# Generation's parameters in turns, ten stored pieces for twelve, and a newly searched order

## The chip, the cores and the metric

One core of a Trainium2 chip. The metric is the device time of one execution in microseconds; a run is one execution. The program is straight-line: every engine (TensorE, here PE, with its weight loads PEld; VectorE, DVE; ScalarE, ACT; GpSimd, POOL; and SyncE, SP, which issues DMAs) has its own list of instructions and takes them in order, and semaphores make one wait for another.

## The reference

Two mixers over the same x (2048 positions of 640 channels), blended by a gate.

```
g = sigmoid((x * gate_w).sum(-1))
# a: attention, 32 heads of 20; each position sees itself and 7 earlier ones, 2 apart
qkv = x @ wqkv;  a = softmax(q . k[s - 2w] / sqrt(20)) . v[s - 2w], w = 0..7;  a = a @ wo
# b: a long convolution whose filter comes from 640 x 192 complex modes
dt = exp(log_dt)
K[d, l] = Re sum_n C[d,n] * exp(dt[d] * A[d,n] * l) * dt[d] * B[d,n]
b = irfft(rfft(x, 4096) * rfft(K, 4096))[:2048] + x * Dskip
out = g * a + (1 - g) * b
```

For each mode, the kernel needs logarithm and angle of the weight C B dt, and the rates dt A_re and dt A_im.

## The kernel before

**Start.** The inputs are loaded. `SSMParams.build` computes the parameters on tiles of 128 partitions x 960 (five channels of 192 modes each), on DVE and ACT: the weight wr, wi; its log size xl; its angle at by an arc tangent of the smaller over the larger of |wr| and |wi|, followed by three corrections by octant; the phase per step tau; the decay per step xa. Each result is split into bf16 pieces that add up to it (`piece`: ACT copies to bf16, the DMA on SP stores it to Sprm in DRAM, DVE subtracts it from the value, and so on). Beside this PE transposes x (`turn`, evicted by `tev`) and makes q, k and v (`late`, five matmuls of 512 columns for one 128 x 512 tile, evicted by `lev` on ACT or DVE). At most two such tiles are open at a time (tb has two buffers).

**Generation.** `KGen` loads pieces from Sprm into L (`L0S` on SP and `L0G` on POOL for the first of ten chunks of channels) and multiplies L by a table of constants Rarg (`arg`, on PE): this gives the arguments of sine and exponential for 32 + 2 x 22 or 32 + 22 steps. The sine's argument is wanted modulo one turn: a large constant (MAGIC) is added in the same matmul, so that the low 16 bits of the f32 sum are the phase in units of 1/65536 turn, read as int16. ACT takes the sine (`act`, scaled by 2 pi / 65536) and the exponential; DVE multiplies them (`pq`), and PE sums over the modes with dense small matmuls (`kmm`), evicted by `fin`. Beside it runs the attention in eight blocks of 256 positions: loads of qc, kc, vc on POOL, products on DVE (`prod`, `pv`), sums on PE (`lg`, `gat`), the exponential on ACT, the output projection (`wo`, evicted by `ga`). POOL also loads rows of x (Usb) for the FFT.

**FFT.** The filter is expanded and both it and x are transformed (`f1`, `fk`, `fu`); then comes `fft_conv`, with a plan of its own, "tail", which the change leaves as it is.

**Order.** Every step is a task of a `Plan`. The string `ORDER["main"]` gives the sequence of all tasks as differences of their numbers, with a letter where a task runs on the engine that isn't its first choice. `Plan.emit` records the tasks in that sequence, and each engine keeps it. It was found by a search, outside of the kernel.

Of the kernel before, what the change touches and what calls it, by code (L numbers as in the profile page):

```python
# [10 lines left out]
ACT = mybir.ActivationFunctionType  # L11
ALU = mybir.AluOpType
# [8 lines left out]
S = 2048  # L21
# [16 lines left out]
def _attn_consts():  # L38
# [443 lines left out]
def _arg_consts():  # L482


    i = np.arange(KI)
    m = np.array(MS)
    sp = np.zeros((64, 4, KI), np.float32)
    sq = np.zeros((64, 4, 2, NM), np.float32)
    ep = np.zeros((64, 4, KI), np.float32)
    eq = np.zeros((64, 4, NM), np.float32)  # L490
    for qq in range(4):
        r = 2 + qq * NPC
        for j in range(3):
            sp[r + j, qq] = 8.0 * i - 124.0
            sq[r + j, qq] = (m % 256)[None]
            sq[r + 5 + j, qq] = (m // 256)[None]
        for j in range(2):
            ep[r + 3 + j, qq] = 8.0 * i
            eq[r + 3 + j, qq] = m
            sq[r + 8 + j, qq] = 1.0  # L500
            eq[r + 10 + j, qq] = 0.5
# [17 lines left out]
class SSMParams:  # L519
# [5 lines left out]
    def build(self, ctx, tc, pl, A_re, A_im, B_re, B_im, C_re, C_im, log_dt, gate_w, at_, pa, xl, wl):  # L525
# [25 lines left out]
        dt2 = pin.tile([128, 5], F32, name="dt2")  # L551
# [11 lines left out]
        for c in (MAGIC, -MAGIC * 65536.0, 1e-36, float(-np.pi / 2)):  # L563
# [8 lines left out]
        def tt(name, o, a, b, alu, rdy=0.0):  # L572
            ap = lambda n: dtB if n == "dtb" else dt2[:].unsqueeze(2).to_broadcast(SH) if n == "dt2" else t[n][:]
# [19 lines left out]
        def wrap(dst, src, mul, tmp):  # L593
            lin(tmp, src, mul / 65536.0, MAGIC)
            lin(tmp, tmp, 65536.0, -MAGIC * 65536.0)
            stt(dst, src, float(mul), tmp, ALU.mult, ALU.subtract)

        def piece(cur, nxt, i):
            k = f"pc{i}"

            def make(_):
                t[k] = pcs.tile(SH, BF16, name="pc")
                SCA.activation(t[k][:], t[cur][:], ACT.Identity)
            op(f"mk{i}", "A", 0.9, make, [cur], [k], acq=["pc"])
# [4 lines left out]
        def split(src, i0, n):  # L609
            bufs = [src, "s0", "s1"][:n] + [None]  # L610
# [723 lines left out]
```

## Time and profile before

| | |
|---|---|
| runs (3) | 351.91, 352.40 and 354.79 us, median 352.4 |
| the profiled execution | 354.43 us |
| its span, first to last instruction | 352.4 us |
| mean granted clock of TensorE | 0.972 |
| busy: PE, DVE, ACT, POOL | 305.6, 307.8, 306.1, 86.6 us |
| table loads of ACT in the first 65 us | 6, each 1.283 us |

Times in the profile are microseconds from the first instruction. A row of the timeline has its start, its length, the engine (SPq and POOLq are the queues that issue DMAs), the line, the operation, output <- inputs, shapes, and the count merged in it; in brackets stands how long the engine had been idle and who released it. "issue" means that it waited for nothing that the profile shows.

### The profile page before, as it was taken

To read this page: it belongs to the slowest core of one execution; us is meant where nothing else is said; L and a number is where in the kernel's file an instruction comes from. 1 tells how busy PE (TensorE), PEld (TensorE's weight loads), DVE (VectorE), ACT (ScalarE), POOL (GpSimd) and SP (SyncE) were. 2 spreads that over 40 slices of the span, in tenths; PEclk is the share of its full clock that TensorE was granted. 3 is DMA by queue.
4 is the path that set the end of the run, shared out by engine and by line. 5 is a ranking of instruction groups with operands and counts; after the bars stand their busy time and mean duration, and the time that the engine had idled before them with its cause. 6 is when DMAs were issued, how large, how long until landed. Compare 5 with 4: busy or idle time off the path is not lost. (4 is left out here: it accounts for less than half of the span.)

```text
span 352.4 us, 11782 instructions
## 1 busy us (share of the span) xinstructions
PE 305.6 (87%) x5051; PEld 182.0 (52%) x5094; DVE 307.8 (87%) x421; ACT 306.1 (87%) x460; POOL 86.6 (25%) x110
## 2 busy tenths in 40 slices
PE   0598989999999999999999699999889989997860
PEld 0444544444454455444545255566567866666750
DVE  5999989889999989999999499999667879999982
ACT  2999983899999999999999499988687979998991
POOL 8912303132030030001413333574011000000052
PEclk9999999999999999999999699999999999998995
DMA  8965685557266074206696594625338236566046
GB/s 261 360 191 154 182 243 138 152 174 233 79 171 227 13 232 134 50 14 190 206 322 168 114 283 123 172 76 162 124 120 264 87 131 196 144 133 113 4 118 182
DMA packets 43373, 56.76 MB, mean 161 GB/s; under 512 B 19514, under 2 KB 35194, under 8 KB 43322
## 3 DMA queue, kind: packets, MB, share of 16 engines
q1 hardware_dynamic: 35136, 30.96, 30.6%
q0 software_dynamic: 7440, 24.45, 23.8%
q8 instruction: 39, 0.64, 0.7%
q10 hardware_dynamic: 746, 0.61, 0.6%
q14 instruction: 12, 0.10, 0.1%
HBM read 36.24 MB, written 19.77 MB: 159 GB/s over the span
## 5 line engine op out<-in xcount | busy, mean ns | idle before, releaser
L288 PE MATMUL tb<-bufA 128*128 128x512 bf16 x273 | 75.2, 392 | 8.0 <-issue 2.9
L752 ACT ACTIVATE big<-ar 128x608 bf16<-128x608 int16 x96 | 59.0, 682 | 6.5 <-PE ar L740 5.2
L740 PE MATMUL ar<-Rarg,L 64*128 64x304 bf16 (+1 forms) x480 | 52.5, 279 | 5.4 <-issue 3.0
L754 ACT ACTIVATE big<-ar 128x864 bf16<-128x864 f32 x60 | 50.3, 920 | 0.1
L336 DVE TENSOR_TENSOR prod<-qc,kc 128x2048 bf16<-128x2048 bf16 x40 | 47.9, 1219 | 2.2 <-PE lg L342 2.0
L402 DVE TENSOR_TENSOR pv<-vc,asb 128x2048 bf16<-128x2048 bf16 x40 | 48.4, 1219 | 1.4 <-PE tb L408 1.3
L288 PEld LDWEIGHTS <-bufA 128*128 128x128 bf16 x300 | 31.6, 122 | 34.7 <-issue 17.1
L791 PEld LDWEIGHTS <-pt 128*32 128x32 bf16 (+1 forms) x2560 | 25.3, 92 | 29.8 <-issue 22.2
L408 PE MATMUL tb<-pv,ident 128*128 128x512 bf16 (+1 forms) x176 | 37.9, 341 | 1.6 <-issue 1.3
L791 PE MATMUL kps<-qq,pt 128*32 128x22 bf16 (+1 forms) x2560 | 36.2, 173 | 1.7 <-issue 1.3
L740 PEld LDWEIGHTS <-L 64*128 64x128 bf16 x480 | 20.7, 94 | 27.7 <-issue 23.0
L774 DVE TENSOR_TENSOR pt<-big 128x1024 bf16<-128x1024 bf16 x48 | 32.2, 686 | 1.6 <-PE kps L791 0.6
L431 PE MATMUL tb<-wo_sb,oT 128*128 128x320 bf16 x160 | 30.7, 311 | 1.3 <-ACT ga L440 1.3
L1126 POOL DMA_DIRECT2D out_dram<-ot x14 | 7.7, 558 | 70.7 <-PE yp L1099 68.8
L458 ACT ACTIVATE sp_u<-fp 128x640 bf16<-128x640 f32 x31 | 23.5, 929 | 0.8 <-PE fp L1008 0.8
L408 PEld LDWEIGHTS <-ident 128*128 128x128 bf16 x192 | 17.0, 98 | 13.1 <-issue 1.6
L458 ACT ACTIVATE sp_k<-fp 128x640 bf16<-128x640 f32 x29 | 22.5, 960 | 1.1 <-PE fp L1008 1.1
L458 ACT ACTIVATE big<-bp 128x1024 bf16<-128x1024 f32 x17 | 16.8, 1026 | 5.7 <-PE bp L1235 5.6
L776 DVE TENSOR_TENSOR qq<-big 128x1408 bf16<-128x1408 bf16 x24 | 21.2, 885 | 0.0
L938 POOL COPY pace<-Usb 32x2 bf16<-32x2 bf16 x7 | 13.9, 1989 | 24.7 <-DMA Usb<-in_A_x_dram 24.7
L458 ACT ACTIVATE prj<-tb 128x512 bf16<-128x512 f32 x25 | 15.5, 618 | 5.1 <-PE tb L288 5.1
L1008 PEld LDWEIGHTS <-PHI 128*128 128x128 bf16 x160 | 15.5, 97 | 8.1 <-issue 1.1
(177 smaller groups left out, 582.9 us busy)
## 6 DMA issues: line engine op xcount, KB each, us to landing
asb<-aS SPq DMA_DIRECT2D x8, 512.0 KB, 4.3
Sprm<-pc SPq DMA_DIRECT2D x12, 240.0 KB, 4.3
L<-Sprm SPq DMA_DIRECT2D x76, 36.0 KB, 2.4
kc<-kS POOLq DMA_DIRECT2D x8, 337.5 KB, 4.8
vc<-vS POOLq DMA_DIRECT2D x8, 337.5 KB, 6.2
xn<-in_A_x_dram SPq DMA_DIRECT2D x4, 640.0 KB, 6.1
qc<-qS POOLq DMA_DIRECT2D x8, 320.0 KB, 4.1
gaS<-ga SPq DMA_DIRECT2D x8, 320.0 KB, 2.5
```

Of the source, the lines that this page charges most:

```text
L288: nc.tensor.matmul(ppf, self.wq[:, which, kt, e::5], self.xT[:, c0 // 1024, kt, c0 % 1024:c0 % 1024 + SC], start=(kt == 0), stop=(kt == NK ...
L336: nc.vector.tensor_tensor(b[e][:], b["qc"][:, e, :].unsqueeze(1).to_broadcast([128, W, C]), win(b["kc"][:, e, :], 0, W, DIL, C), ALU.mult)
L402: nc.vector.tensor_tensor(b["pv", e][:, :, k, :].rearrange("p w (b t) -> p w b t", t=64), for_e, aw, ALU.mult)
L408: nc.tensor.matmul(b["op", e][:, 0:n, :], ident[:], b["pv", e][:, w, 0:n, :], start=(w == 0), stop=(w == W - 1))
L431: nc.tensor.matmul(apf[:, :320], b["oT"][:, e, i * 128:(i + 1) * 128], wo_sb[:, e, hf * 320:(hf + 1) * 320], start=(e == 0), stop=(e == 4))
L458: nc.scalar.activation(o, i, ACT.Identity)
L740: nc.tensor.matmul(ar[:, g2, a0:a0 + ncol], L[rows, sb, gp, l0:l0 + 128], R[rows, c0:c0 + ncol], start=True, stop=True, tile_position=(64 ...
L752: nc.scalar.activation(dst[:, 2 * gp:2 * gp + 2, sub, :], ar[:].bitcast(I16)[:, :, 0:2 * SW:2], ACT.Sin, scale=SCL)
L754: nc.scalar.activation(dst[:, 2 * gp:2 * gp + 2].rearrange("p g s n -> p g (s n)"), ar[:, :, 0:2 * EW], ACT.Exp)
L774: nc.vector.tensor_tensor(pt[:, :, k, :], gg[:, :, ::-1] if k else gg, e1, ALU.mult)
L776: nc.vector.tensor_tensor(qq[:], trg[:, :, KI:].rearrange("p a (v m) -> p a v m", v=2), exq[:, :, KI:].unsqueeze(2).to_broadcast([128, 32, ...
L791: nc.tensor.matmul(kps[32 * g:32 * g + 32, h, NM * ql:NM * ql + NM], pt[rows, k, v, :], qq[rows, k, v, :], start=(g not in started), stop= ...
```

## The change

The unit of the phase becomes a turn. dt is multiplied once by 1/(2 pi) (`dtc`, 128 x 5), so that the phase is in turns from the start, and "modulo one turn" is: add and subtract MAGIC in one pass, and subtract (`nearest`). `wrap`, two passes and a third, goes, and so does the separate split of 256 tau (`x1`). The phase's pieces are digits of fixed units, 2^-8, 2^-16, 2^-24, each made by DVE by adding and subtracting MAGIC times the unit (`digit`), and a fourth piece for what is left; the other pieces (two each of xl, xa and at) are made by ACT or DVE. The log size takes dt in as lnd, half the logarithm of the size being added to it. The angle comes from the half angle: wi / (|w| + |wr|), with |w| = exp(0.5 ln |w|^2) and the division as exp(-ln); one correction instead of three. Rarg's rows are arranged to match, and ten pieces are stored per mode instead of twelve. `ORDER["main"]` is new; each of its places differs.

```
-NPC = 12
+NPC = 10
...
-        for j in range(3):
-            sp[r + j, qq] = 8.0 * i - 124.0
-            sq[r + j, qq] = (m % 256)[None]
-            sq[r + 5 + j, qq] = (m // 256)[None]
+        for j in range(4):
+            sp[r + j, qq] = 65536.0 * (8.0 * i - 124.0)
+            sq[r + j, qq] = 65536.0 * (m if j else m % 256)[None]
...
-        def wrap(dst, src, mul, tmp):
-            lin(tmp, src, mul / 65536.0, MAGIC)
-            lin(tmp, tmp, 65536.0, -MAGIC * 65536.0)
-            stt(dst, src, float(mul), tmp, ALU.mult, ALU.subtract)
+        def nearest(o, a, unit):
+            c = MAGIC * unit
+            op(f"near_{o}", "D", 0.62, lambda _: V.tensor_scalar(t[o][:], t[a][:], c, c, ALU.add, ALU.subtract), [a], [o])
+
+        def digit(cur, nxt, i, unit):
+            k, c = f"pc{i}", MAGIC * unit
+
+            def make(_):
+                t[k] = pcs.tile(SH, BF16, name="pc")
+                V.tensor_scalar(t[k][:], t[cur][:], c, c, ALU.add, ALU.subtract)
+            op(f"mk{i}", "D", 0.62, make, [cur], [k], acq=["pc"])
+            op(f"sp{i}", "S", 0.36, lambda _: nc.sync.dma_start(Sv[:, :, i, :], t[k][:]), [k], [f"S{i}"], dma=1.1)
+            op(f"rs{i}", "D", 1.07, lambda _: V.tensor_tensor(t[nxt][:], t[cur][:], t[k][:], ALU.subtract), [cur, k], [nxt])
...
-            op(f"mk{i}", "A", 0.9, make, [cur], [k], acq=["pc"])
+            op(f"mk{i}", "AD", {"A": 0.9, "D": 0.62}, make, [cur], [k], acq=["pc"])
...
         def phase():
-            tt("tau", "tau", "aim", "dtb", ALU.mult, rdy=9.6)
-            wrap("tau", "tau", U16, "s0")
-
-        def ratio():
-            stt("t0", "ax", 1e-30, "ay", ALU.max, ALU.max)
...
-            tt("s0", "s0", "t0", "s1", ALU.mult)
-            stt("t0", "s0", 2.0, "s1", ALU.subtract, ALU.mult)
-            tt("t1", "t1", "ax", "ay", ALU.min)
-            stt("t1", "t1", -1.0, "t0", ALU.mult, ALU.mult)
-            act("at", "t1", ACT.Arctan, "atan")
+            tt("tau", "tau", "aim", "dtc", ALU.mult, rdy=9.6)
+            nearest("x1", "tau", 1.0)
+            tt("tau", "tau", "tau", "x1", ALU.subtract)
...
+        def half():
+            op("act_ay", "A", 0.9, lambda _: SCA.activation(t["ay"][:], t["xl"][:], ACT.Exp, scale=0.5), ["xl"], ["ay"], table="exp")
+            tt("ay", "ay", "ay", "ax", ALU.add)
+            op("act_t0", "A", 0.9, lambda _: SCA.activation(t["t0"][:], t["ay"][:], ACT.Ln, bias=bias[1e-36]), ["ay"], ["t0"], table="ln")
+            op("act_t1", "A", 0.9, lambda _: SCA.activation(t["t1"][:], t["t0"][:], ACT.Exp, scale=-1.0), ["t0"], ["t1"], table="exp")
+            tt("t1", "t1", "wi", "t1", ALU.mult)
+            act("at", "t1", ACT.Arctan, "atan")
+            op("stt_xl", "D", 1.07, lambda _: V.scalar_tensor_tensor(t["xl"][:], t["xl"][:], 0.5, lnd[:].unsqueeze(2).to_broadcast(SH), ALU.mult, ALU.add), ["xl", "lnd"], ["xl"])
...
+        def digits():
+            for i, (a, b) in enumerate((("tau", "s0"), ("s0", "s1"), ("s1", "s0"))):
+                digit(a, b, i, 2.0 ** (-8 * i - 8))
+            piece("s0", None, 3)
...
-        for step in [weights, phase, squares, st[0], ratio, size, st[1], st[2], lambda: wrap("x1", "tau", 256.0, "t0"), sl[0], sl[1], angle1, sx[0],
-                     sx[1], angle2, sx[2], lambda: tt("xa", "xa", "are", "dtb", ALU.mult, rdy=19.0), sa[0], angle3, sa[1], sp[0], sp[1]]:
+        for step in [weights, phase, size, half, digits, lambda: two("xl", "ax", 8), angle, start, lambda: two("at", "x1", 6),
+                     lambda: tt("xa", "xa", "are", "dtb", ALU.mult, rdy=19.0), lambda: two("xa", "ay", 4)]:
```

What the new order does to the engines' lists is shown at three places. The first is the head of DVE's list (wr, wi: the weight; tau: the phase; dt and dtc: the small tiles made from dtb, which ACT makes from log_dt). Before:

```order
L574 TENSOR_TENSOR wr<-cre,bre 128x960 [waits DMAHW1_49,DMAHW0_49]
L574 TENSOR_TENSOR t_144<-cim,bim 128x960 [waits DMAHW3_49,DMAHW2_49]
L574 TENSOR_TENSOR wr<-wr,t_144 128x960 [waits DVE_49]
L624 TENSOR_TENSOR dt_139<-dtb 128x5 [waits Activation_49]
L574 TENSOR_TENSOR t_145<-cim,bre 128x960
L574 TENSOR_TENSOR tau<-aim,dtb 128x960 [waits DMAHW0_49]
```

and now:

```order
L628 TENSOR_SCALAR dtc<-dtb 128x5 [waits Activation_49]
L573 TENSOR_TENSOR wr<-cre,bre 128x960 [waits DMAHW1_49,DMAHW0_49]
L573 TENSOR_TENSOR t_145<-cim,bim 128x960 [waits DMAHW3_49,DMAHW2_49]
L573 TENSOR_TENSOR t_146<-cim,bre 128x960
L573 TENSOR_TENSOR wr<-wr,t_145 128x960 [waits DVE_49]
```

The small tile, which waits for ACT, moved from fourth place to the first. The second place is the end of the parameters on DVE (pc: a piece; at: the angle; prj: a tile of q, k or v; prod: the first block's products). Before:

```order
L607 TENSOR_TENSOR s_155<-xa,pc 128x960 [waits DVE_49,Activation_49]
L460 CAST prj<-tb 128x512 [waits DMAHW6_49,DMAHW7_49,DMAHW1_49,PE_49]
L580 SCALAR_TENSOR_TENSOR at<-at,t_145 128x960 [waits Activation_49]
L460 CAST prj<-tb 128x512 [waits PE_49]
L607 TENSOR_TENSOR s_155<-at,pc 128x960 [waits Activation_49]
```

and now:

```order
L573 TENSOR_TENSOR at<-at,t_145 128x960 [waits DVE_49]
L460 CAST pc<-at 128x960 [waits DMAHW2_49,DVE_49]
L615 TENSOR_TENSOR x_152<-at,pc 128x960 [waits DVE_49]
L460 CAST pc<-x_152 128x960 [waits DMAHW5_49,DMAHW1_49,DVE_49]
L460 CAST prj<-tb 128x512 [waits DMAHW7_49,DMAHW6_49,PE_49]
```

The last pieces are now made by DVE itself, where each step waited for ACT. The third place is the first argument matmul in PE's list (lg: the first block's logits, hi and lo the two halves of minus its maximum, at its exponentials; bufA: the weights of q, k, v). Before:

```order
L370 MATMUL lg<-at,ident 128x64
L288 LDWEIGHTS bufA
L288 MATMUL tb<-bufA 128x512
L740 LDWEIGHTS L_165
L740 MATMUL ar<-Rarg,L_165 128x304
```

and now:

```order
L362 MATMUL lg<-hi,ident 128x512
L362 LDWEIGHTS ident
L362 MATMUL lg<-lo,ident 128x512
L288 LDWEIGHTS bufA
L288 MATMUL tb<-bufA 128x512
L743 LDWEIGHTS L_162
L743 MATMUL ar<-Rarg,L_162 128x304
```

The first block's sum over exponentials, which stood ahead of the argument, now stands behind it, and so do 20 more of the L288 matmuls: 122 of them are ahead of it where 142 were. ACT's list has 461 instructions for 469, DVE's 415 for 423; ACT_TABLE_LOAD stands on ACT 19 times for 17.

More of the change, by code (lines that the diff above doesn't have):

```diff
@@ L467 @@
 MAGIC = 12582912.0
-U16 = 65536.0 / (2.0 * np.pi)
 CQ = 8
 NCH = 80 // CQ
-NPC = 12
+NPC = 10
 KI = 32
@@ L492, in _arg_consts @@
         r = 2 + qq * NPC
-        for j in range(3):
-            sp[r + j, qq] = 8.0 * i - 124.0
-            sq[r + j, qq] = (m % 256)[None]
-            sq[r + 5 + j, qq] = (m // 256)[None]
+        for j in range(4):
+            sp[r + j, qq] = 65536.0 * (8.0 * i - 124.0)
+            sq[r + j, qq] = 65536.0 * (m if j else m % 256)[None]
         for j in range(2):
[L498 to L501, printed above, removed]
+            ep[r + 4 + j, qq] = 8.0 * i
+            eq[r + 4 + j, qq] = m
+            sq[r + 6 + j, qq] = 65536.0
+            eq[r + 8 + j, qq] = 1.0
     sp[0] = MAGIC; sq[0] = MAGIC
@@ L550, in build @@
         dtb = pin.tile([128, 5], BF16, name="dtb")
-        dt2 = pin.tile([128, 5], F32, name="dt2")
+        dtc = pin.tile([128, 5], F32, name="dtc")
+        lnd = pin.tile([128, 5], F32, name="lnd")
         dtB = dtb[:].unsqueeze(2).to_broadcast(SH)
@@ L562, in build @@
         bias = {}
-        for c in (MAGIC, -MAGIC * 65536.0, 1e-36, float(-np.pi / 2)):
+        for c in (1e-36, 0.5):
             bc = pin.tile([128, 1], F32, name=f"bc{len(bias)}")
@@ L572, in tt @@
         def tt(name, o, a, b, alu, rdy=0.0):
-            ap = lambda n: dtB if n == "dtb" else dt2[:].unsqueeze(2).to_broadcast(SH) if n == "dt2" else t[n][:]
+            ap = lambda n: dtB if n == "dtb" else dtc[:].unsqueeze(2).to_broadcast(SH) if n == "dtc" else t[n][:]
             op(name, "D", 1.07, lambda _: V.tensor_tensor(t[o][:], ap(a), ap(b), alu), [a, b], [o], rdy=rdy)
@@ L591, in lin, with make @@
             op(f"lin_{o}", "AD", {"A": 0.9, "D": 0.62}, fn, [a], [o])
-        def wrap(dst, src, mul, tmp):
-            lin(tmp, src, mul / 65536.0, MAGIC)
-            lin(tmp, tmp, 65536.0, -MAGIC * 65536.0)
-            stt(dst, src, float(mul), tmp, ALU.mult, ALU.subtract)
+        def nearest(o, a, unit):
[9 more added lines that the diff above has]
+            op(f"rs{i}", "D", 1.07, lambda _: V.tensor_tensor(t[nxt][:], t[cur][:], t[k][:], ALU.subtract), [cur, k], [nxt])
         def piece(cur, nxt, i):
             k = f"pc{i}"
-            def make(_):
+            def make(e):
                 t[k] = pcs.tile(SH, BF16, name="pc")
-                SCA.activation(t[k][:], t[cur][:], ACT.Identity)
-            op(f"mk{i}", "A", 0.9, make, [cur], [k], acq=["pc"])
+                evict(nc, e, t[k][:], t[cur][:])
+            op(f"mk{i}", "AD", {"A": 0.9, "D": 0.62}, make, [cur], [k], acq=["pc"])
             op(f"sp{i}", "S", 0.36, lambda _: nc.sync.dma_start(Sv[:, :, i, :], t[k][:]), [k], [f"S{i}"], dma=1.1)
@@ L607, in piece @@
                 op(f"rs{i}", "D", 1.07, lambda _: V.tensor_tensor(t[nxt][:], t[cur][:], t[k][:], ALU.subtract), [cur, k], [nxt])
-        def split(src, i0, n):
-            bufs = [src, "s0", "s1"][:n] + [None]
-            return [lambda i=i: piece(bufs[i], bufs[i + 1], i0 + i) for i in range(n)]
         for n_, v in zip(("t0", "t1", "wr", "wi", "ax", "ay", "tau", "x1", "xa", "xl", "at", "s0", "s1"), (t0, t1, wr, wi, ax, ay, tau, x1, xa, xl_, at, s0, s1)):
@@ L622, in weights @@
             tt("wi", "wi", "wi", "t1", ALU.add)
-            act("ay", "wi", ACT.Abs)
-            op("dt2", "D", 0.16, lambda _: V.tensor_tensor(dt2[:], dtb[:], dtb[:], ALU.mult), [], ["dt2"])
+            op("dtc", "D", 0.12, lambda _: V.tensor_scalar(dtc[:], dtb[:], float(0.5 / np.pi), None, ALU.mult), [], ["dtc"])
         def phase():
-            tt("tau", "tau", "aim", "dtb", ALU.mult, rdy=9.6)
-            wrap("tau", "tau", U16, "s0")
-        def ratio():
-            stt("t0", "ax", 1e-30, "ay", ALU.max, ALU.max)
-            op("act_s0", "A", 0.9, lambda _: SCA.activation(t["s0"][:], t["t0"][:], ACT.Ln), ["t0"], ["s0"], table="ln")
-            op("act_s1", "A", 0.9, lambda _: SCA.activation(t["s1"][:], t["s0"][:], ACT.Exp, scale=-1.0), ["s0"], ["s1"], table="exp")
-            tt("s0", "s0", "t0", "s1", ALU.mult)
-            stt("t0", "s0", 2.0, "s1", ALU.subtract, ALU.mult)
-            tt("t1", "t1", "ax", "ay", ALU.min)
-            stt("t1", "t1", -1.0, "t0", ALU.mult, ALU.mult)
-            act("at", "t1", ACT.Arctan, "atan")
@@ L640, in squares, with size @@
-        def squares():
+            tt("tau", "tau", "aim", "dtc", ALU.mult, rdy=9.6)
+            nearest("x1", "tau", 1.0)
+            tt("tau", "tau", "tau", "x1", ALU.subtract)
+        def size():
             act("xl", "wr", ACT.Square)
             act("xa", "wi", ACT.Square)
-        def size():
             tt("xl", "xl", "xl", "xa", ALU.add)
-            tt("xl", "xl", "xl", "dt2", ALU.mult)
             op("act_xl", "A", 0.9, lambda _: SCA.activation(t["xl"][:], t["xl"][:], ACT.Ln, bias=bias[1e-36]), ["xl"], ["xl"], table="ln")
-        def angle1():
-            tt("t0", "t0", "ay", "ax", ALU.is_gt)
-            stt("t1", "at", float(np.pi / 4), "t0", ALU.subtract, ALU.mult)
-            stt("at", "t1", -2.0, "at", ALU.mult, ALU.add)
@@ L654, in angle2 @@
-        def angle2():
-            lin("t1", "at", 1.0, float(-np.pi / 2))
-            stt("t1", "wr", 0.0, "t1", ALU.is_lt, ALU.mult)
-            stt("at", "t1", -2.0, "at", ALU.mult, ALU.add)
-        def angle3():
-            stt("t1", "wi", 0.0, "at", ALU.is_lt, ALU.mult)
-            stt("at", "t1", -2.0, "at", ALU.mult, ALU.add)
-            lin("t0", "tau", 124.0, 0.0)
-            stt("at", "at", float(U16), "t0", ALU.mult, ALU.add)
-            wrap("at", "at", 1.0, "t1")
-        st, sx, sa, sl, sp = split("tau", 0, 3), split("x1", 5, 3), split("xa", 3, 2), split("xl", 10, 2), split("at", 8, 2)
@@ L666, in build @@
-        for step in [weights, phase, squares, st[0], ratio, size, st[1], st[2], lambda: wrap("x1", "tau", 256.0, "t0"), sl[0], sl[1], angle1, sx[0],
-                     sx[1], angle2, sx[2], lambda: tt("xa", "xa", "are", "dtb", ALU.mult, rdy=19.0), sa[0], angle3, sa[1], sp[0], sp[1]]:
+            op("lnd", "A", 0.24, lambda _: SCA.activation(lnd[:], dtb[:], ACT.Ln), [], ["lnd"], table="ln")
+        def half():
[6 more added lines that the diff above has]
+            op("stt_xl", "D", 1.07, lambda _: V.scalar_tensor_tensor(t["xl"][:], t["xl"][:], 0.5, lnd[:].unsqueeze(2).to_broadcast(SH), ALU.mult, ALU.add), ["xl", "lnd"], ["xl"])
@@ new lines, in angle, with start @@
+        def angle():
+            lin("t1", "at", -2.0 / np.pi, 0.5)
+            stt("t1", "wr", 0.0, "t1", ALU.is_lt, ALU.mult)
+            stt("at", "at", float(1.0 / np.pi), "t1", ALU.mult, ALU.add)
+        def start():
+            stt("at", "tau", 124.0, "at", ALU.mult, ALU.add)
+            nearest("t0", "at", 1.0)
+            tt("at", "at", "at", "t0", ALU.subtract)
+        def digits():
+            for i, (a, b) in enumerate((("tau", "s0"), ("s0", "s1"), ("s1", "s0"))):
+                digit(a, b, i, 2.0 ** (-8 * i - 8))
+            piece("s0", None, 3)
@@ L668, in build, with two @@
+        def two(src, rest, i):
+            piece(src, rest, i)
+            piece(rest, None, i + 1)
+        for step in [weights, phase, size, half, digits, lambda: two("xl", "ax", 8), angle, start, lambda: two("at", "x1", 6),
+                     lambda: tt("xa", "xa", "are", "dtb", ALU.mult, rdy=19.0), lambda: two("xa", "ay", 4)]:
             step()
```

86 rows, old and new, of the table ORDER are left out of this document.

## The prediction

> **What bounds the kernel now.** First the busy shares of the page, then a table of the span in stages, then the timeline of the first 65 us.
>
> ```profile
> PE 305.6 (87%) x5051; PEld 182.0 (52%) x5094; DVE 307.8 (87%) x421; ACT 306.1 (87%) x460; POOL 86.6 (25%) x110
> ```
>
> Three engines stand at the same 87%, so the average names no bound. By stage (length, then busy us and instructions of PE, its weight loads, DVE, ACT, POOL, then the granted clock, DMA share and GB/s):
>
> ```profile
> 20.00:30.00 10.00, 8.72 (x41) 4.43 (x41) 9.54 (x11) 9.94 (x13) 1.35 (x2) 1.00 0.40 121
> 30.00:40.00 10.00, 8.81 (x61) 5.33 (x62) 9.72 (x10) 10.00 (x15) 1.76 (x2) 1.00 0.77 229
> 40.00:50.00 10.00, 8.78 (x109) 5.34 (x109) 8.68 (x10) 9.21 (x12) 2.60 (x3) 1.00 0.84 225
> 50.00:60.00 10.00, 9.38 (x54) 3.99 (x54) 9.79 (x17) 4.15 (x6) 3.21 (x5) 1.00 0.43 101
> 65.00:85.00 20.00, 19.07 (x172) 7.84 (x172) 16.91 (x24) 19.78 (x28) 6.76 (x8) 1.00 0.65 192
> 85.00:105.00 20.00, 18.96 (x436) 9.70 (x440) 18.41 (x27) 19.13 (x32) 3.87 (x5) 1.00 0.51 139
> 105.00:125.00 20.00, 18.81 (x472) 9.72 (x477) 18.86 (x25) 19.53 (x30) 0.85 (x1) 1.00 0.41 139
> 125.00:145.00 20.00, 19.54 (x457) 10.75 (x462) 19.38 (x23) 19.88 (x33) 3.50 (x4) 1.00 0.56 161
> 145.00:165.00 20.00, 19.13 (x382) 10.12 (x382) 19.29 (x26) 19.82 (x35) 1.58 (x2) 1.00 0.18 49
> 165.00:185.00 20.00, 18.59 (x389) 9.86 (x392) 18.95 (x36) 19.94 (x30) 5.79 (x7) 1.00 0.84 275
> 185.00:205.00 20.00, 16.59 (x373) 8.06 (x374) 13.91 (x20) 14.56 (x27) 6.50 (x11) 0.83 0.64 153
> ```
>
> From 65 to 185 us ACT is idle for 1.9 us of 120 and PE for 5.9: this stretch, in which the filter is generated, is full. From 20 to 50 ACT and DVE are nearly full with the parameters while PE loses 3.7 us; from 50 to 60 ACT is busy for 4.15 only. So what a faster parameter stage is worth is read from where generation starts:
>
> ```profile
> 50.80 1.00 ACT L603 ACTIVATE pc<-s 128x960 bf16<-128x960 f32 x1 [1.55 <-DMA Sprm<-pc]
> 55.75 4.64 SPq L712 DMA_DIRECT2D L<-Sprm  x10
> 63.39 0.43 PE L740 MATMUL ar<-Rarg,L 64*128 64x304 bf16 x4
> 65.07 7.32 ACT L752 ACTIVATE big<-ar 128x608 bf16<-128x608 int16 x12
> 282.82 0.70 PE L1008 MATMUL fp<-bufA,PHI 128*128 128x320 bf16 x4 [0.91 <-ACT bufA L458]
> ```
>
> The last piece is made at 51.80, the tables L are fetched 3.95 us later, the first argument matmul stands at 63.39 and the first sine at 65.07. The FFT part, whose order is not changed, starts at 282.82: the middle is 219.4 us long.
>
> **The change, part by part.** DVE's parameter instructions first: a three-operand pass when it needs nothing new, when it needs the result just in front of it, and a one-source pass.
>
> ```profile
> 9.00 1.15 DVE L574 TENSOR_TENSOR tau<-aim,dtb 128x960 f32<-128x960 bf16 x1
> 10.07 1.15 DVE L574 TENSOR_TENSOR wi<-cre,bim 128x960 f32<-128x960 bf16 x1
> 23.66 1.15 DVE L574 TENSOR_TENSOR s<-t,s 128x960 f32<-128x960 f32 x1
> 24.85 1.16 DVE L580 SCALAR_TENSOR_TENSOR t<-s,s 128x960 f32<-128x960 f32 x1
> 27.24 0.66 DVE L588 TENSOR_SCALAR t<-tau 128x960 f32<-128x960 f32 x1
> 27.93 0.66 DVE L588 TENSOR_SCALAR t<-t 128x960 f32<-128x960 f32 x1
> 14.02 1.22 DVE L460 CAST bufA<-ar 128x1024 bf16<-128x1024 f32 x1
> 22.00 0.69 DVE L460 CAST pv<-tb 128x512 bf16<-128x512 f32 x1
> ```
>
> Start to start that is 1.07, 1.19 and 0.58 to 0.69 us; I use 1.11 and 0.63. Before, DVE has 33 passes with a second tensor and 4 with one source; after, 23 and 10 (a nearest integer twice, three digits, one line, four copies to bf16): 10 x 1.11 less and 6 x 0.63 more, **7.3 us less on DVE**. The three digits and four copies write bf16 from f32 in SBUF, a form that this trace does not show. Bounds: 0.63 like the f32 passes here, 1.15 like the eviction of 1024 f32 above, scaled to 960. Source and size are those of the 0.63 rows, so I take that; at the upper end the seven cost 3.6 us more. The Trainium skill (VectorE: DVE Perf Modes, "The perf-mode tier table") says that one-source passes on f32 in SBUF run at twice the rate of two-source passes and that any PSUM operand drops a tier; 0.66 against 1.15 us here agrees, and by it the lower bound is the right one.
>
> ACT made all 12 pieces and half of the lines: 24 passes before, 11 after. One costs 0.90 start to start, and a table load 1.30:
>
> ```profile
> 18.02 1.28 ACT L632 ACT_TABLE_LOAD   x1
> 19.32 1.00 ACT L632 ACTIVATE s<-t 128x960 f32<-128x960 f32 x1
> 24.00 0.99 ACT L603 ACTIVATE pc<-xl 128x960 bf16<-128x960 f32 x1
> 24.90 0.59 ACT L458 ACTIVATE pv<-tb 128x512 bf16<-128x512 f32 x1
> 6.75 0.21 ACT L553 ACTIVATE dtb<-ldt 128x5 bf16<-128x5 bf16 x1 [2.26 <-DMA ldt<-in_B_log_dt_dram]
> ```
>
> 13 x 0.90 goes, 2 x 1.30 comes since logarithm and exponential now take turns (ln, exp, ln, exp, arc tangent where it was ln, exp, arc tangent): **9.1 us less on ACT**. The Trainium skill (ScalarE: Activation LUTs, "What ACT_TABLE_LOAD costs") speaks against this edit: it puts a change of table set at 2.66 us, a drain included, so two more would be 5.3 us and the arc tangent 2.7 us later. Here the pass starts 1.30 us after the load did, and no drain is seen; I give that rule 2 in 100, at 346.7 + 2.7 = 349.4.
>
> Now the chain to the first argument matmul. The changed order puts dtc, which needs dtb, **first** on DVE; before, three large passes stood ahead of the small one. dtb is ready at 6.96, held by its load, so DVE's first pass starts at 7.1 and not at 4.41: a new wait of 2.7 us with all of DVE behind it. From there DVE has 23 x 1.11 + 10 x 0.63 + the large eviction at 1.13 + four small ones at 0.60 (the row of 0.69 less the 0.08 by which all of these overlap) = 35.4, and the last piece is ready at 42.5; I add 0.7 for late5's eviction, whose PE work cannot start before ACT's fourth large eviction at about 18.4. That is 43.2 against 51.8. ACT is not later: from the square of wi at 14.75 to the end of the arc tangent stand 8 passes and 3 large evictions at 0.90, 4 table loads at 1.30 and 6 small evictions at 0.48, 18.0 us, so 32.8 and some 34 with short waits for PE; DVE by its own sum needs the arc tangent at 34.1. With ten stores for twelve and L cut from 48 to 40 rows, nothing on SP grows; I count that as nothing, hidden under DVE's passes. L at 43.2 + 3.95 = 47.2, its landing some 4 us later.
>
> Three things then meet at the first argument:
>
> ```profile
> 50.48 2.35 DVE L336 TENSOR_TENSOR prod<-qc,kc 128x2048 bf16<-128x2048 bf16 x2
> 59.59 0.23 DVE L358 SCALAR_TENSOR_TENSOR lo<-mx,hi 128x64 bf16<-128x64 f32 x1
> 17.14 3.57 PE L288 MATMUL tb<-bufA 128*128 128x512 bf16 x8 [0.84 <-ACT bufA L458]
> 60.46 2.32 PE L288 MATMUL tb<-bufA 128*128 128x512 bf16 x10
> ```
>
> - L itself: about 51.5.
> - DVE: the new order has the first block's softmax maximum ahead of the argument on PE. From the first product to that maximum's low part took 59.82 - 50.48 = 9.3 us with two evictions among it that now stand in front: 43.2 + 9.3 = 52.5, and a microsecond of PE: 53.5.
> - PE: ten matmuls of 512 took 2.32 us with their drain, 0.216 each. PE had 142 of them ahead of the first argument and now has 122, so 4.3 us less. It began them at 17.14 and now begins at 18.4. With all of its old gaps it would reach the first argument at 63.39 - 4.3 + 1.3 = 60.4. Those gaps, the 4.3 us of idle from 20 to 60 and small ones inside the rows (the first eight above take 3.57 us where 1.73 would do), are waits for evictions by ACT and DVE, which have 16 us less to do. Without any gap, 122 x 0.216 and some 6.6 us of transposes, gate, logits and sums would end at 51.4.
>
> The middle of PE's two ends is 55.9, and DVE says 53.5; I take **55.5**, 7.9 us before 63.39.
>
> What is given back: the 20 matmuls, 4.3 us, now stand inside the middle, where PE has 5.9 us to spare in 120 and ACT almost none. Ends: nothing, if they fall into PE's gaps, and 4.3, if PE is the bound throughout. Neither row is nearer, since both engines stand above 95%; I take 2.2. The rest of the middle (evictions that change sides, loads on POOL in another order, the eight tiny Dk loads later) I count as nothing: the work is the same, and POOL's queue is covered, being busy 22.4 us of those 120 by the table. If that cover is gone somewhere, a load late by one landing is some 2 us.
>
> Sum: -7.9 + 2.2 = **-5.7**. The profiled execution took 354.43 us (span 352.4 and 2.0 around it), so 348.7 by its own time; the runs' median is 2.0 lower, 352.4, and the forecast for a median is **346.7**.
>
> **The rivals.** The last row of the stage table holds a dip of its own: PE stops in front of an argument matmul, waits for nothing that is shown, and then the granted clock is 0.50 while DVE waits.
>
> ```profile
> 197.51 0.41 PE L740 MATMUL ar<-Rarg,L 64*128 64x304 bf16 x1 [2.96 <-issue]
> 198.00:200.00 2.00, 2.00 (x25) 0.78 (x23) 0.00 (x0) 1.12 (x2) 0.18 (x1) 0.50 0.08 19
> 203.02 0.53 DVE L1219 CAST E<-kps 128x352 bf16<-128x352 f32 x1 [5.29 <-PE kps L791]
> ```
>
> One such stop is worth 5.3 us by DVE's wait. Nothing in the change removes it, but it comes where row loads and dense small matmuls meet, and both move.
>
> - **The stop is gone**: 346.7 - 5.3 = 341.4. For it: it belongs to a coincidence. Against it: the same loads still meet the same matmuls. 0.12.
> - **Nothing is gained, because PE's queue was the bound at 63.39, not L.** For it:
>
> ```profile
> L<-Sprm POOLq DMA_DIRECT2D x4, 36.0 KB, 2.2
> ```
>
> The last of L's loads was issued at about 58 and lands 2.2 us later, before 61, yet the argument came at 63.39 with PE busy for 9.38 of the ten us before 60. If PE keeps its gaps (60.4) and 4.3 is given back, the sum is -3.0 + 4.3 = +1.3, 353.7; halfway to the forecast still within 1%. Against it: those gaps end in waits for ACT and DVE, and these are relieved. 0.20. That the change would not shorten the parameters at all I leave out: the passes are counted.
> - **Slower: the stop multiplies.** PE has less slack in the middle, attention and generation run closer together, and the row loads on POOL meet denser small matmuls. Each further stop costs 5.3; one gives 352.0, which nobody could tell from no change, and two decide: 346.7 + 10.6 = 357.3. For it: one stop is there already, at a DMA share above 0.6. Against it: only one so long in the whole trace. 0.11.
>
> **How the numbers follow.** The forecast has 0.55, with 343.5 to 350 as its own range (first argument between 53.5 and 58.5, 0 to 4.3 given back, the bf16 copies at their upper end), the three rivals 0.12, 0.20 and 0.11, the table rule 0.02. Leaving out the slower case and the far ends of the two others, the range is 341 to 353.5. A measurement of this kernel tells some 1% (3.5 us) from no change: 348.9 and 355.9 are the borders. Faster takes 0.48 of the forecast and the missing stop, 0.60; within 1% the forecast's rest, the second rival and the table rule, 0.29; slower 0.11.
>
> **What would show it.** In the profile after: DVE's first large pass near 7.1, behind dtc; the copies to bf16 near 0.66; the last piece near 43; the tables L fetched near 47; the first argument matmul near 55.5 and the first sine a microsecond and a half later; the FFT part's first matmul near 277; the middle some 2 us longer than 219.4. I am wrong if DVE waits for ACT's chain of five functions in the thirties, if the first argument is at 60 with L long there, or if PE shows more than one stop of three microseconds.

## The result, and the profile after

The median went from 353.26 us (4 runs, 351.91 to 354.79) to **343.62** (4 runs, 341.04 to 343.85): ratio 0.971, interval 0.964 to 0.977. The forecast was 346.7, faster. The profiled execution took 343.48 us, its span 341.7 (before: 354.43 and 352.4).

The timeline of the changed kernel, for the steps that the prediction named:

```profile
7.00 0.93 DVE L628 TENSOR_SCALAR dtc<-dtb 128x5 f32<-128x5 bf16 x1 [6.02 <-ACT dtb L552]
7.08 1.16 DVE L573 TENSOR_TENSOR wr<-cre,bre 128x960 f32<-128x960 bf16 x1
...
18.52 0.66 DVE L601 TENSOR_SCALAR pc<-tau 128x960 bf16<-128x960 f32 x1
...
34.26 0.66 DVE L587 TENSOR_SCALAR t<-at 128x960 f32<-128x960 f32 x1 [0.20 <-ACT at L582]
...
43.03 0.66 DVE L460 CAST pc<-x 128x960 bf16<-128x960 f32 x1
46.38 4.62 SPq L715 DMA_DIRECT2D L<-Sprm  x12
54.11 0.23 DVE L358 SCALAR_TENSOR_TENSOR lo<-mx,hi 128x64 bf16<-128x64 f32 x1
54.39 0.38 PE L362 MATMUL lg<-lo,ident 128*128 128x512 bf16 x1
55.13 0.43 PE L743 MATMUL ar<-Rarg,L 64*128 64x304 bf16 x4
56.80 3.69 ACT L755 ACTIVATE big<-ar 128x608 bf16<-128x608 int16 x6
...
271.98 0.70 PE L1011 MATMUL fp<-bufA,PHI 128*128 128x320 bf16 x4 [1.01 <-DVE om L975]
```

DVE's large passes begin at 7.08 behind the small tile, six of the seven passes to bf16 take 0.65 to 0.66 (one takes 0.94), DVE waits 0.20 us for the arc tangent, the last piece is done at 43.7, L is fetched from 46.4, the first argument matmul is at 55.13 (before 63.39) and the FFT part's first at 271.98 (before 282.82). PE's waits from 17 to 56 us (waiting tile <- releaser: us, times, longest):

```profile
PE tb L288 <- ACT pv L458: 0.9, 2, 0.4
PE ar L206 <- ACT bufA L458: 0.3, 1, 0.3
PE tb L288 <- ACT prj L458: 0.2, 1, 0.2
```

That is 1.4 us, where the same view had 4.5 before: the evictions come in time now. Two stretches of the middle (length; busy PE, weight loads, DVE, ACT, POOL, each with its count; granted clock, DMA share, GB/s):

```profile
125.00:145.00 20.00, 19.97 (x404) 10.21 (x401) 19.38 (x27) 19.78 (x30) 0.00 (x0) 1.00 0.29 82
185.00:205.00 20.00, 19.99 (x511) 10.49 (x509) 19.93 (x26) 19.41 (x34) 7.62 (x11) 1.00 0.96 259
```

PE is now the fullest engine, and the stretch that held the stop of 3.6 us and the clock of 0.83 has neither. One smaller stop is left, at another place, among the small generation matmuls:

```profile
99.40 0.23 PE L794 MATMUL kps<-qq,pt 64*32 64x22 bf16 x9 [1.27 <-issue]
```

By stages the span, 10.7 us shorter, splits so: start to the first argument -8.3; from there to the FFT part's first matmul 219.4 before, 216.9 now, -2.5; the rest 69.6 and 69.7.

### The profile page after: what moved, and what is told of

Same layout as the page of the kernel before. It is cut to its first block, busy times and chain, and to the rows that moved or that the text cites. A ratio compares the mean times of both kernels' runs of the same rounds, so it can differ in the third digit from the quotient of the medians.

```text
span 341.7 us, 11769 instructions
## 1 busy us (share of the span) xinstructions
PE 306.2 (90%) x5094; PEld 180.7 (53%) x5094; DVE 299.0 (88%) x413; ACT 297.7 (87%) x452; POOL 83.9 (25%) x110
## 5 line engine op out<-in xcount | busy, mean ns | idle before, releaser
L288 PE MATMUL tb<-bufA 128*128 128x512 bf16 x300 | 79.6, 390 | 1.3 <-ACT pv L458 0.9
L755 ACT ACTIVATE big<-ar 128x608 bf16<-128x608 int16 x96 | 59.8, 686 | 3.3 <-PE ar L743 2.6
L743 PE MATMUL ar<-Rarg,L 64*128 64x304 bf16 (+1 forms) x480 | 49.4, 276 | 0.6
L402 DVE TENSOR_TENSOR pv<-vc,asb 128x2048 bf16<-128x2048 bf16 x40 | 48.1, 1216 | 0.0
L288 PEld LDWEIGHTS <-bufA 128*128 128x128 bf16 x300 | 31.1, 122 | 29.0 <-issue 10.9
L408 PE MATMUL tb<-pv,ident 128*128 128x512 bf16 (+1 forms) x192 | 40.6, 345 | 0.8 <-DVE pv L402 0.8
L431 PE MATMUL tb<-wo_sb,oT 128*128 128x320 bf16 x160 | 28.8, 301 | 0.0
L458 ACT ACTIVATE prj<-tb 128x512 bf16<-128x512 f32 x28 | 17.2, 614 | 4.8 <-PE tb L288 4.8
L431 PEld LDWEIGHTS <-oT 128*128 128x128 bf16 x160 | 13.5, 97 | 7.0 <-issue 1.7
```

The source lines that it names most:

```text
L288: nc.tensor.matmul(ppf, self.wq[:, which, kt, e::5], self.xT[:, c0 // 1024, kt, c0 % 1024:c0 % 1024 + SC], start=(kt == 0), stop=(kt == NK ...
L402: nc.vector.tensor_tensor(b["pv", e][:, :, k, :].rearrange("p w (b t) -> p w b t", t=64), for_e, aw, ALU.mult)
L408: nc.tensor.matmul(b["op", e][:, 0:n, :], ident[:], b["pv", e][:, w, 0:n, :], start=(w == 0), stop=(w == W - 1))
L431: nc.tensor.matmul(apf[:, :320], b["oT"][:, e, i * 128:(i + 1) * 128], wo_sb[:, e, hf * 320:(hf + 1) * 320], start=(e == 0), stop=(e == 4))
L458: nc.scalar.activation(o, i, ACT.Identity)
L743: nc.tensor.matmul(ar[:, g2, a0:a0 + ncol], L[rows, sb, gp, l0:l0 + 128], R[rows, c0:c0 + ncol], start=True, stop=True, tile_position=(64 ...
```

## Experiments on the start: what sets the first argument

The kernels are compared with one of the two kernels, before (medians 351.7 to 353.7 beside them) or after (343.62). After ran beside none of them, and its own four runs spread from 341.04 to 343.85, so a difference of a microsecond from it says little by itself.

**dtc later.** The only new wait that the order brought is taken away: dtc goes back behind the first passes.

```
 ORDER["main"], as tasks on DVE
-dtc, wr, t0, t1, wr, ...
+wr, t0, t1, wr, wi, dtc, tau, ...
```

> The changed kernel with the small pass dtc moved from the head of DVE's list to just in front of the pass that needs it. Theory: DVE's list sets the first argument matmul; DVE starts at 4.4 instead of 7.1, the last piece is ready near 41, the first argument comes 1.5 to 2.7 us earlier (53 for 55.1), and at least half of that is left at the end: 1 to 2.5 us faster than the changed kernel, 341 to 342.5. Rival: PE's queue is as late as DVE's list there; the first argument stays within 0.5 us of 55.1 and the time within 0.5 us.

Measured: 343.65 us, no change. DVE began at 4.38 instead of 7.08, yet the first argument came later:

```profile
56.21 0.43 PE L744 MATMUL ar<-Rarg,L 64*128 64x304 bf16 x4
```

```profile
PE tb L289 <- ACT pv L459: 2.5, 3, 1.4
```

PE waited 2.5 us for ACT's evictions, where it waited 0.9, and its granted clock was 0.50 from 46.1 to 49.5:

```profile
46.00:48.00 2.00, 1.78 (x10) 0.75 (x9) 1.87 (x6) 0.18 (x1) 1.56 (x3) 0.52 0.16 39
```

DVE lost most of its earlier start to waits for PE and ACT: the last piece was done at 43.13, only 0.56 us earlier. So the wait of 2.7 us at the head of DVE, which the prediction charged in full on DVE's path, costs nothing in the end. That PE's queue is what holds the first argument is not shown by this kernel alone, because of its slower clock; the next one shows it at a clock of 1.00.

**Three small passes.** Three of DVE's two-source passes are done on 20 of 960 elements (so the angles are not reduced).

```
-stt("t1", "wr", 0.0, "t1", ALU.is_lt, ALU.mult)             # 128 x 960
+V.scalar_tensor_tensor(t["t1"][:, :, 0:4], t["wr"][:, :, 0:4], 0.0, ...)
 (likewise at - t0 in start(), and the rest behind piece 6)
```

> After, with three two-source DVE passes of the parameters (the half-turn test, the subtraction of the nearest integer in the starting angle, the rest behind piece 6) done on 20 of 960 elements, so that these angles are not reduced: some 3.0 us less on DVE. The last piece near 40.7 instead of 43.7, L some 3 us earlier. My theory after the second experiment (PE's queue has no wait left between 20 and 55 and is itself the bound at 55.1): the first argument between 54 and 55.5, median 342.5 to 343.9. Rival (the chain through DVE and L still sets the first argument): first argument near 52.2, median 340.6.

Measured: 343.29 us, the first argument at 55.04 where after has 55.13. The last piece was done 3.0 us earlier, at 40.7, and two covers took that. The waits on SP, and DVE's timeline:

```profile
SPq L716 <- DMA Sprm<-pc: 4.9, 1, 4.9
```

```profile
43.26 0.69 DVE L460 CAST prj<-tb 128x512 bf16<-128x512 f32 x1 [2.60 <-PE tb L288]
```

L was issued at 46.37 (after: 46.38): the stores of the last two pieces, issued at 39.9 and 40.7, landed no earlier. Their packets moved from 42.7 to 45.6, until 44.2 beside a load of attention rows on POOL; that this load held them up fits, but was not tried. And DVE then waited 2.6 us for PE, whose own waits from 17 to 56 us were 2.2 us. PE's queue is the bound at 55; a shorter parameter chain gains nothing there.

**Four more passes.** The other direction: one subtraction is done five times.

```
-lambda _: V.tensor_tensor(t[nxt][:], t[cur][:], t[k][:], ALU.subtract)
+lambda _: [V.tensor_tensor(...) for _ in range(5 if i == 6 else 1)]
```

> After, with the subtraction behind piece 6 done five times: four more DVE passes of 128 x 960 at 1.07 to 1.11 us, 4.3 to 4.4 us more on DVE between the angle and the last pieces. My theory (the middle has a fixed length and what comes ahead of the first argument matmul is paid one for one): DVE's softmax maximum reaches PE at 54.3 in after and PE's own queue at 55.1, so DVE has at most 0.8 us to spare; the first argument at 58.5 to 59.6, the span 3.4 to 4.4 us longer, the median 347.0 to 348.0. Rival (PE's queue holds the first argument, DVE has slack): first argument at 56 or before, median within 1 us of 343.6. Second rival (a late first argument is made up again in the middle): first argument near 59, the FFT part still near 272, median within 1.5 us of 343.6.

Measured: 347.09 us (346.76 to 349.58), +3.5. The first argument is at 60.55 (+5.4), the FFT part at 276.61 (+4.6). The start's size was missed by a microsecond. PE, which had not waited for DVE before, now did, and then ran at half the clock, which was 0.50 from 48.0 to 54.8:

```profile
60.55 0.43 PE L743 MATMUL ar<-Rarg,L 64*128 64x304 bf16 x4
```

```profile
PE tb L288 <- DVE prj L460: 2.8, 1, 2.8
```

```profile
50.00:52.00 2.00, 2.00 (x6) 0.66 (x5) 2.00 (x3) 0.15 (x1) 0.00 (x0) 0.50 0.45 123
```

PE went on at 49.52, so 5.3 us of its work ran at half the clock; by an estimate from these times that lost 2.6 us, and with the wait of 2.8 it makes the 5.4. A late start is paid to the end almost in full (4.6 of 5.4); an earlier DVE gives nothing. DVE's softmax maximum (54.34) and PE's queue (55.13) meet within a microsecond in after.

**Twelve stored.** Two pieces are stored and fetched twice, as many rows as before (their rows of Rarg are zero).

```
-NPC = 10
+NPC = 12
-nc.sync.dma_start(Sv[:, :, i, :], t[k][:])
+[nc.sync.dma_start(Sv[:, :, j, :], t[k][:]) for j in ((i, i + 2) if i > 7 else (i,))]
```

> After, with twelve pieces stored and fetched again as in the kernel before (two pieces are stored twice, their rows of the fixed table of the argument matmul are zero): two more stores of 0.51 us on SP and L loads of 36 instead of 30 KB. Theory (PE's queue sets the first argument at 55.1, and L has some two microseconds to spare): first argument at 55.1 to 56.1, median 343.0 to 345.0. Rival (L sets it): two stores and larger loads behind them, first argument at 56.5 to 58, median 345 to 347.

Measured: 343.34 us, first argument at 55.23, L issued at 47.04 instead of 46.38. Ten stores for twelve bring nothing, as the prediction had it.

**New parameters in the old order.** The sequence is that of before; the places of its parameter tasks are filled with the new tasks in their new sequence.

```
 ORDER["main"]: all other tasks in before's sequence
-parameter tasks of before
+parameter tasks of after, spread over the same places
```

> The changed kernel's parameters in the old order: all other tasks keep the sequence of before, and the new parameter tasks take the places of the old ones, one by one from the first. Theory: the shorter parameters are needed but PE's list decides when generation starts; with 142 matmuls of q, k, v ahead the first argument comes at 58 to 60, L long landed, the middle keeps its stop near 194 less 4, and the time is 348 to 351. Rival 1, the parameters do it all: first argument near 55, time 344 to 346. Rival 2, without the new order nothing is gained: first argument after 62, time 352 or more.

Measured: 357.83 us (356.76 to 358.49), 5.4 slower than before, against what I expected and as the second rival had it. DVE's waits name it:

```profile
DVE t L573 <- ACT t L646: 5.0, 1, 5.0
```

This is what the prediction gave as its first way to be wrong, a wait for ACT's chain of five functions; in the old order it comes true, between 31 and 36 us, and the first argument is at 67.81.

**Old parameters in the new order**, made the other way round.

```
 ORDER["main"]: all other tasks in after's sequence
-parameter tasks of after
+parameter tasks of before, spread over the same places
```

> The kernel before's parameters in the new order: all other tasks in the new sequence, the old parameter tasks spread over the places of the new ones. Theory: DVE and ACT have their 16 us more, so the last piece is ready near 51 to 52, the first argument 8 us after the changed kernel's, at 62 to 64, and the time is 349 to 353. Rival, the order does it: PE reaches the first argument before 58, time 344 to 347.

Measured: 364.90 us (363.87 to 365.94), 12.4 slower than before, first argument at 75.66. PE stands behind ACT, which has all twelve pieces again:

```profile
PE tb L289 <- ACT pv L459: 10.7, 6, 4.1
```

Among these waits its granted clock was 0.50 for 17 us of the start (24.2 to 31.0, 41.3 to 48.1 and 65.2 to 68.6), so the lateness is not the waits alone.

Neither half gains by itself (+5.4, +12.4; together -9.6). The places here were filled mechanically, so a better mixture is not excluded.

## Experiments on the middle

**Thirty more matmuls.** The prediction charged 2.2 of 4.3 us for the 20 L288 matmuls that moved into the middle. Here 30 of them are done twice; 4 of the copies come ahead of the first argument, 26 behind.

```
+if sc > 1 and kt == 0:
+    nc.tensor.matmul(ppf, self.wq[:, which, kt, e::5], self.xT[...], start=True, stop=True)
 nc.tensor.matmul(ppf, self.wq[:, which, kt, e::5], self.xT[...], start=(kt == 0), stop=(kt == NKT - 1))
```

> After, with the first matmul of 30 projection tiles done twice: 30 more matmuls of 512 columns with their weight loads, 30 x 0.216 = 6.5 us of PE, nearly all of it between the first argument matmul and the FFT part. Prediction's term: 20 such matmuls that moved into the middle were to cost 2.2 of 4.3 us, so 30 cost 3.3; the accounting (2.8 of 4.3) gives 4.2; with PE busy 19.9 of 20 us through most of the middle the upper end is 6.5. Rival (ACT or DVE bounds the middle, PE's work is hidden): under 1.5 us. So theory: middle 220.2 to 223.4 instead of 216.9, median 346.9 to 350.1; rival: median 343.6 to 345.1.

Measured: 348.60 us (347.38 to 350.50), +5.0.

```profile
57.13 0.43 PE L746 MATMUL ar<-Rarg,L 64*128 64x304 bf16 x4
...
279.02 0.70 PE L1014 MATMUL fp<-bufA,PHI 128*128 128x320 bf16 x4 [1.01 <-DVE om L978]
```

The profile is of the slowest of the four runs (350.50). In it the first argument is 2.0 later and the middle is 221.9, 5.0 longer: 0.19 us for each of 26 matmuls that last 0.216. The median is 1.9 below that run; if all of this is taken off the middle, an estimate, the price is 0.12. PE is at or near the bound of the middle; by these prices the 20 matmuls are worth 2.4 to 3.9 us, in the upper half of the prediction's 0 to 4.3.

## Experiments on the stop

**The stop moved.** 64 weight loads and one-column matmuls are added to the kernel before, at the head of the gate.

```
+for _ in range(64):
+    nc.tensor.matmul(gz[:, 0, 16:17], self.xT[:, 0, 0, 0:128], self.gw[:, 0:1], start=True, stop=True)
```

> The kernel before with 64 extra weight load and matmul pairs (one column each, into an unused column) at the head of the gate's step, near 43 us; nothing else. Theory: PE stops for 3 us near 194 because the next 256 instructions of its list arrive late; the stop stands at an instruction whose number is 194 more than a multiple of 256. 128 instructions more move that edge by half a block, so no stop is left in front of this argument matmul, and unless the new edges meet the same DMA crowd the time falls by 3 to 5 us, to 348 to 351 (the extra pairs cost at most 2 us, in a stretch where PE has gaps). Rival: the stop belongs to this matmul and what it reads; then it stays in front of the same matmul, the clock dips as before, and the time is that of before or 1 to 2 us more.

Measured: 352.17 us (12 runs) beside 352.48, ratio 1.002 (0.999 to 1.006). The fall of 3 to 5 us did not come. The long stop was not there; two shorter ones were, and the clock stayed at 1.00 up to 202.4. Behind the second it was 0.50 until 205.9:

```profile
195.01 0.32 PE L793 MATMUL kps<-qq,pt 64*32 64x22 bf16 x24 [0.54 <-issue]
200.93 0.42 PE L742 MATMUL ar<-Rarg,L 64*128 64x304 bf16 x3 [1.26 <-issue]
...
202.00:204.00 2.00, 1.67 (x40) 0.88 (x40) 2.00 (x4) 1.94 (x4) 1.03 (x3) 0.61 0.08 22
```

The first argument was at 64.27, the middle 216.9. Against the second profile of before (below: 63.73, 217.4) the shorter stops gave half a microsecond and the added work took it.

**What stands at the stops.** Counting PE's instructions by the program's list, every stop named here lies at an instruction whose number is 194 above a multiple of 256. The page has a queue for instructions:

```profile
q8 instruction: 39, 0.64, 0.7%
```

39 packets of 16 KB, one about every 256 instructions of PE. The Trainium skill (Runtime: NRT & Kernel Launch, "Instruction fetch mechanics") says that an engine fetches its list in blocks of 256 instructions by a DMA queue of its own, while it executes the block before, and that this is mostly hidden. The packets agree with the block. In the kernel before, two blocks stop PE for over a microsecond; most of the others are hidden. Times from the traces (us), block by block:

```
kernel                 edge before   its packet         edge reached   PE goes on   stop
before                    190.56     194.66 to 195.91      194.25        197.85     3.60
before                    242.64     244.89 to 246.05      246.13        247.57     1.44
after                      94.17      97.01 to  97.93       97.94         99.40     1.46
after                     190.77     193.82 to 194.97      196.53        196.53     none
before, again             190.90     194.46 to 195.64      194.59        197.24     2.65
before, 32 pairs          191.05     191.90 to 192.83      195.43        195.43     none
before, 128 pairs         196.87     200.57 to 201.82      200.56        203.35     2.79
after, 16 pairs           185.24     187.76 to 188.63      188.54        190.37     1.83
```

An edge is the place in PE's list where one block ends and the next begins. In these rows a packet starts 0.9 to 4.1 us after PE passed the edge before, and PE goes on 1.5 to 1.9 us after it ended, where it had to wait. In the rows with a stop PE was through with the 256 instructions in 3.3 to 3.8 us, with many small generation matmuls and their weight loads among them; then the packet can be too late.

All 14 traces, counted in the same way, agree. Each idle stretch of PE of over 0.4 us that is put down to "issue" lies at such an edge, and at none of 435 edges between 66 and 285 us did PE go on sooner than 1.26 us after the packet's end. The packet's start lies 2.1 us behind the edge before (median of 128) where the DMA share of the next 2 us is 0.9 or more, and 0.6 us (median of 175) where it is under 0.5. That the other transfers delay it is the obvious reading; no kernel here changed them alone. The last four kernels test the rest.

**The kernel before, again.** No edit.

> The kernel before, unchanged, once more. Theory (the stop of PE at 194 is a late fetch of its instructions, which depends on when the other transfers happen, and so is in some executions and not in others): the place of the long stop, its length or both differ from the first profile, and the executions spread over some 3 to 5 us, with a middle of 214 to 219.4. Rival (the stop belongs to the program): a stop of 3.6 us at the same matmul, middle 219.4.

Measured: 352.92 us (10 runs, 350.60 to 357.37) beside 353.67; middle 217.4.

```profile
197.03 0.29 PE L740 MATMUL ar<-Rarg,L 64*128 64x304 bf16 x1 [2.14 <-issue]
```

The stop is at the same instruction, as the rival had it, but 2.65 us long instead of 3.60, as the theory had it: the place is fixed by the program, the length by when the packet comes.

**32 pairs**, 64 instructions, in the kernel before (the edit above with 32).

> The kernel before with 32 more weight loads and one-column matmuls in the gate, ahead of everything disputed: 64 more instructions on PE, some 0.5 us. Theory (PE stops when the next 256 of its own instructions have not arrived; the places are every 256th instruction of its list, whatever stands there): near 194 the stop stands 64 instructions earlier in the program, not in front of the argument matmul where it stood twice, but among the small generation matmuls ahead of it, at the instruction whose number is again 5826 of PE's list. Rival (the stop belongs to that argument matmul and its operands): the stop stands in front of the same argument matmul, at 194.7, as in the kernel before. Time by both: 351 to 355.

Measured: **348.95 us** (348.16 to 349.43) beside 352.56, ratio 0.988 (0.984 to 0.992). More work, and faster. That the time would stay was wrong, and so was the new place of the stop: there is none near 194 and none near 246 (an idle stretch of 0.71 us at an edge, at 111, is left).

```profile
194.00:196.00 2.00, 1.98 (x75) 1.17 (x75) 1.74 (x3) 2.00 (x5) 0.00 (x0) 1.00 1.02 217
```

```profile
277.58 0.70 PE L1010 MATMUL fp<-bufA,PHI 128*128 128x320 bf16 x4 [0.91 <-ACT bufA L460]
```

The first argument is at 64.00, so the middle is 213.6 without the long stops and 219.4 with them: in the first profile of before they cost 5.8 us, in the second 3.8.

**128 pairs**, one whole block (the edit above with 128).

> The kernel before with 128 such pairs, 256 instructions, 1.8 us of PE in the gate. Theory: a whole block of instructions, so the blocks end at the same places of the program as in the kernel before, and the stop returns in front of the same argument matmul, 1 to 2 us later (195 to 196.5), 2 to 3.6 us long, with the granted clock at 0.5 to 0.6 behind it; middle 217.4 to 219.4, median 353.5 to 356. Rival (the places do not follow the instruction numbers, the shift only disturbs): stop elsewhere or none over 2 us.

Measured: 358.23 us (357.20 to 359.40), ratio 1.014 (1.010 to 1.019). Both stops of before are back, in front of the same two instructions, each 256 later in the list:

```profile
203.14 0.29 PE L742 MATMUL ar<-Rarg,L 64*128 64x304 bf16 x1 [2.28 <-issue]
...
252.16 0.24 PE L793 MATMUL kps<-qq,pt 64*32 64x22 bf16 x11 [0.92 <-issue]
```

The middle is 218.1, as expected. The time is 2 us above what I expected, because the 128 pairs are themselves a block that is burnt too fast. PE's waits from 10 to 70 us, and a window of that stretch:

```profile
PE ar L223 <- issue: 1.9, 1, 1.9
```

```profile
48.00:52.00 4.00, 2.06 (x22) 1.19 (x23) 0.00 (x0) 1.00 (x1) 0.00 (x0) 0.51 0.96 241
```

The edit made a stop of its own, the first argument came at 69.29, and this is the rest.

**16 pairs in the kernel after** (the same edit with 16), a place chosen from its trace for a stop.

> After with 16 more weight loads and one-column matmuls in the gate: 32 more instructions on PE, some 0.25 us. By after's trace this puts a block of 256 PE instructions between 186.3 and 189.7, 3.3 us, the shortest that any shift by a multiple of 32 gives between 60 and 270, in a stretch with the DMA share near 0.96; block fetches there end 2.7 to 4.2 us after the edge before and PE goes on some 1.5 us later. Theory (how the list falls into blocks decides on the stops, whatever the program): the stop at 98 goes or moves, one of 1 to 2.5 us comes at 189.5 to 192, the middle 217 to 219.5, the median 344.5 to 347. Rival (the stops of the kernel before came from its own order of work, after is free of them): no stop over 1.3 us in the middle, median 343.3 to 344.3.

Measured: 345.01 us (344.33 to 345.99), 1.4 above after's 343.62; the middle is 219.0.

```profile
190.37 0.23 PE L796 MATMUL kps<-qq,pt 64*32 64x22 bf16 x9 [1.63 <-issue]
...
274.03 0.70 PE L1013 MATMUL fp<-bufA,PHI 128*128 128x320 bf16 x4 [1.01 <-DVE om L977]
```

```profile
192.00:194.00 2.00, 2.00 (x50) 0.81 (x46) 1.14 (x2) 1.13 (x3) 1.43 (x3) 0.50 0.91 260
```

One of 1.83 us came at 190, where the theory put it. The stop at 98 is gone too, but the shift need not be the reason: dtc later, four more passes, three small passes and twelve stored have PE's list as after has it, the same block at the same speed (3.77 us), and no stop there, because its packet started within 0.2 us of the edge and not 2.84 us behind it. So the list sets where a stop can stand, and the packet's time whether it does. Stops are not a matter of the order of before alone.

## Why the prediction was right, and where it was wrong

- **DVE's and ACT's parts: right.** 7.1 and 7.08; the passes to bf16 last 0.66 (but for one), as the f32 ones do; last piece 43.2 and 43.69; L 47 and 46.4. DVE waits 0.20 us for the arc tangent, behind all the added table loads, so the rival by the table rule falls.
- **The first argument: right**, 55.5 and 55.13, -7.9 and -8.3. It was taken between PE without gaps (51.4) and with all old gaps (60.4), and that the middle of the two was so near is in part luck. PE's waits in the start are 1.4 us, so most gaps went with their causes. The second rival named PE's queue as the bound, as it is in after, but had its gaps stay. That DVE's wait for dtb has its price here was wrong in mechanism: the kernel with dtc later shows none.
- **Ten stores for twelve at nothing: right** (343.34).
- **What is given back: right within its range.** 2.2 was taken of 0 to 4.3. Against before without the long stops (213.6) after's middle is 3.3 longer. Its own stop of 1.46 is worth less than its length: the three kernels with the same list on PE and no stop of over a microsecond (dtc later, four more passes, twelve stored) have middles of 216.7, 216.1 and 216.6, so 2.5 to 3.1 are given back. By the price of a matmul in the middle it is 2.4 to 3.9.
- **The stop: the term that was mis-sized.** The forecast carried it over in full; the rival without it, 341.4, had 0.12. It went, and with the shorter one at 246 it was worth 5.8 us in the profile that the sum was made against, where the prediction had 5.3 for the long one alone. -8.3, -5.8 and +3.3 make -10.8; the span shrank by 10.7. That this sum closes proves nothing, since 213.6 stands in both parts of the middle; what carries it is the kernel with 32 pairs. The step that failed is "nothing in the change removes it": the change takes instructions from ahead of it in PE's list and moves others, and so sets anew where the blocks end. The argument against its going, the same loads and the same matmuls, named the wrong cause. So the direction and the start were foreseen, and that 343.62 still lies inside the forecast's own range, 0.12 above its lower end, is luck.
- So of 9.6 us, some 4 are the blocks: before with 32 pairs is at 348.95 with half a microsecond of added work, and after's median is 5.3 below that. After's last stop is worth 0.1 to 0.8 us, by the three middles above.

## What to carry to other kernels

When an engine stops with no releaser in front of dense small instructions, count its list: stops at instruction numbers that differ by multiples of 256 were here its own instruction fetch, and 64 instructions more ahead of them moved the time by a per cent with almost no change in the work. Compare two orders of such a kernel at more than one alignment before crediting the order. And where two chains meet within a microsecond, as DVE's and PE's here at 55 us, shortening one of them alone gave nothing, while lengthening it was paid almost in full. Look at the granted clock beside each wait: in four more passes half the clock cost about as much as the wait itself.

## What the runs showed that was not expected

PE's instruction fetch, above. And the granted clock behind a stop: it stayed at 1.00 behind 1.27 to 1.46 us (three small passes at 196, before at 246, after at 98), and was 0.50 behind 1.57 us (64 pairs at 201) and behind 1.83 to 3.60 us, for 3.4 us in four of these cases and for 6.8 in the others (the longest stop and the one that the 128 pairs made among them). A stop is not the only way to it: in dtc later the clock fell at 46.1, behind 80 matmuls of one column each and an idle stretch of 0.22 us. Whether a long stop costs more than its length is open: the stops of before are 5.0 us long in the first profile and cost 5.8, 3.8 long in the second and cost 3.8.
